# New TensorE piece lengths in an attention planner, and expert 0's block 10 finished in the next stage's order

## The chip, the cores and the metric

The kernel runs on one core of one Trainium2 chip. The metric is device time in microseconds (us) from one launch, the median of several runs. The core's engines each follow their own list of instructions in order: TensorE (PE in the profile, with its weight loads as PEld), VectorE (DVE), ScalarE (ACT), GpSimd (POOL) and SyncE (SP), which here only issues DMA transfers.

## The reference, cut to what matters

Three layers follow each other. Inputs are q, k, v and f_logit of shape (4, 8, 768, 48); all is fp32.

```python
f = 1.0 / (1.0 + np.exp(-f_logit))
for t in range(S):
    state = f[:, :, t, :, None] * state + np.einsum('bhd,bhe->bhde', k[:, :, t], v[:, :, t])
    y[:, :, t] = np.einsum('bhd,bhde->bhe', q[:, :, t], state)
# x = y as (3072, 384)
logits = x @ w_gate
P = np.exp(logits - logits.max())
for _ in range(8):
    P /= P.sum(1, keepdims=True) + 1e-09
    P /= P.sum(0, keepdims=True) + 1e-09
    P *= N / E
for e in range(E):                      # 8 experts, F = 1024
    out += P[:, e:e + 1] * (np.maximum(x @ w1[e], 0.0) @ w2[e])
# second layer: (x @ w_a) * (x @ w_b) @ w_out, inner width 1536
```

The normalisation of P runs over all 3072 tokens, so no expert's result can be weighted before the last token's gate logits are known.

## The kernel before, in words

**Two stages.** The attention stage works through 24 steps of 128 tokens (function `attention`, `NSTEP = 24`). The main stage then does the experts (`front`, `back`), and after them the second layer, over three groups of 1024 tokens. Products are fp32 precision made of fp32r pieces: each operand is split into a high part and a low part, and a product takes three matmuls.

**A step of attention.** TensorE's part is a row of short pieces: three transposes of f, q and k (`tr`, L463), the score products `m0`, `m8`, `m16`, `m32` (L506, L518, L557, L570) over blocks of growing width, a transpose of k (`kt`, L582), two state updates (`kv`, L607) and the output (`ym`, L641). Between them VectorE scales q and k for the next level (L529, L531, L577), copies the finished scores under a mask (L550 after `m0`, L543 after the others), and keeps the state (L632, L634). The order of adding makes the first of the copies at L543 wait for `m16`, which writes the same bank as `m8`. ScalarE does the exponentials of f (L468 to L473), copies k (L588), copies the state into place (L622) and moves `ym`'s result out (L650). SyncE rearranges that result into x (L657, six small transfers), and ScalarE and VectorE split x into its high and low part (L670, L671). Two sets of buffers let one step overlap the next.

**Filling work.** While attention waits, TensorE runs expert 0 on blocks of 256 tokens as soon as their two steps are done (function `expert0`): first seven products x times w1 of nine matmuls of 256 columns each (L326), then two products h times w2 of 21 matmuls of 384 columns each (L338), whose results ScalarE moves out (L721) and stores (L723). Below the nine-matmul groups are called F and the 384-column matmuls G. There are twelve blocks. Blocks 0 to 10 are planned into the attention stage as filling work, block 11 into the main stage, since its x comes last. The gates (`logits`, six small matmuls at L681 and a reduction at L686) follow each step's x; the last step's gates are planned into the main stage, where the normalisation of P (`sinkhorn`, L752 to L776) waits for them.

**What sets the order.** A class `Plan` takes every operation with a priority, an engine, a cost, and the keys that it reads and writes. `order` then lists the operations by a time that it keeps for each engine: an operation becomes ready when those that it depends on have ended, plus a gap, and each engine takes the ready one of best priority. In the attention stage TensorE alternates between attention's pieces and filling work: each attention piece of cost c adds `SHARE * c` to an account and each filling piece takes its cost from it; a switch to filling work costs `TURN` more. The order of every engine's list in each stage comes from this one pass; each stage has its own `Plan` and starts its times at zero.

```python
plan.add(prio, PE, .75, [f"x{s % 4}", "wgs"], [kl], lambda: lg(psl))
...
op(PE, .53 * n, hk + wk, [km, "E0o"], partial(
    gemm_t, psm[:, :DM], hs[fs], ws[fs], tt * 128, part == 0, part == 3), 0.0, fill)
...
if i % 2 == 1 and i + 1 < NSTEP:
    expert0(plan, i // 2, 1000 * (i + 1), "M", p_M, True)
...
logits(plan, NSTEP - 1, -4000, "R", p_R[:2])
expert0(plan, NSTEP // 2 - 1, E0_AT, "R", p_R[:2], False)
```

The last two lines are the head of the main stage's list. `x_take` there loads further sums of x (`z<-xf0d` on SyncE), splits them on ScalarE (`xsh`) and on VectorE or GpSimd (`xsl`).

Of the kernel before, what the change touches and what calls it, by code (L numbers as in the profile page):

```python
# [84 lines left out]
class Plan:  # L85
# [6 lines left out]
    GAP = 0.2  # L92
    MOST, DEBT = 2.0, 0.9
    SAME = 0.13
    TURN = 0.19
    COLD = 10.0

    def __init__(self, gap=GAP, hold=GAP, same=SAME, over=0.0):
# [25 lines left out]
    def order(self, share):  # L124
# [56 lines left out]
def kernel(  # L181
# [249 lines left out]
    def attention(s):  # L431
# [34 lines left out]
        op(PE, .44, [f"natf{z}"], [kf], lambda: tr("f", psf))  # L466
# [8 lines left out]
        op(PE, .44, [f"natq{z}"], [kq], lambda: tr("q", psq))  # L475
        kk_, psk = take("T", p_T)
        op(PE, .44, [f"natk{z}"], [kk_], lambda: tr("k", psk))
# [30 lines left out]
        op(PE, 1.1, [bqk, bkk], [a0k], m0)  # L508
# [13 lines left out]
        op(PE, .95, [f"q3{z}", f"k3{z}"], [a1k], m8)  # L522
# [38 lines left out]
        op(PE, .85, [f"q3{z}", f"k3{z}"], [a1k], m16)  # L561
# [11 lines left out]
        op(PE, .73, [f"q3{z}", f"k3{z}"], [a1k], m32)  # L573
# [11 lines left out]
        op(PE, .46, [f"k3{z}"], [ko], lambda: kt(pso))  # L585
# [28 lines left out]
        for c in range(2):  # L614
            kc, psc = take("O", p_O)
            op(PE, .55, [knk, f"vn{z}"], [kc], lambda c=c, psc=psc: kv(c, psc))
# [31 lines left out]
        op(PE, 1.2, [f"Xq{z}", f"Xa{z}", f"Yv{z}", f"Ys{z}"], [ky], lambda: ym(psy))  # L648
# [25 lines left out]
    def logits(plan, s, prio, nm, bufs):  # L674
# [10 lines left out]
        plan.add(prio, PE, .75, [f"x{s % 4}", "wgs"], [kl], lambda: lg(psl))  # L685
# [3 lines left out]
    def expert0(plan, b, prio, nm, bufs, fill):  # L689
# [7 lines left out]
        for ft in range(NF0):  # L697
# [13 lines left out]
        for tt in range(EB // 128):  # L711
            km, psm = take(nm, bufs)
            for part in range(4):
                n = min(2, NF0 - 2 * part)
                hk = [f"h{x}{ft}" for ft in range(part * 2, part * 2 + n) for x in "hl"]
                fs = slice(part * 2, part * 2 + n)
                wk = [f"e0o{part // 2}{x}" for x in range(e0_f[part // 2])]
                op(PE, .53 * n, hk + wk, [km, "E0o"], partial(
                    gemm_t, psm[:, :DM], hs[fs], ws[fs], tt * 128, part == 0, part == 3), 0.0, fill)
# [59 lines left out]
    for i in range(NSTEP):  # L779
# [3 lines left out]
        if i % 2 == 1 and i + 1 < NSTEP:  # L783
            expert0(plan, i // 2, 1000 * (i + 1), "M", p_M, True)
# [328 lines left out]
    w2d = {}  # L1113
    logits(plan, NSTEP - 1, -4000, "R", p_R[:2])
# [100 lines left out]
```

## Time and profile before

| what | value |
|---|---|
| median of 3 runs | 2245.74 us (2245.48 to 2248.01) |
| the profiled execution, its own time | 2248.24 us |
| its span, first to last instruction | 2246.5 us |
| PE, PEld, DVE, ACT, POOL busy | 97%, 88%, 74%, 44%, 43% of the span |
| TensorE's granted clock, mean | 0.987 |
| chain that ended last | PE 82%, DVE 9%, DMA 4%, ACT 2% |

The profile counts an engine as busy while an instruction of its own runs; a granted clock of 1.00 is the higher of TensorE's two levels (2.4 GHz), 0.50 the lower (1.2 GHz). The shares are means over two stages with different limits, so the sections below read each stage by itself.

### The profile page before, as it was taken

The page shows a single profiled execution, that of the slowest core. Times are in us where ns is not written, and L with a number is a line of the kernel's source. Part 1 is how long each engine was busy: PE and PEld are TensorE (multiplying, and loading weights), DVE is VectorE, ACT ScalarE, POOL GpSimd, SP SyncE. Part 2 cuts the span into 40 slices and gives each one's busy share as a digit, 9 for nine tenths or more (in the row PEclk, how much of TensorE's full clock was granted, in tenths as well). Part 3 has the DMA queues.
Part 4 walks back from the last instruction along what each step waited for, and adds up shares of the span by engine and source line. Part 5 has one row for each costly group of instructions (what it writes and reads, how often), then busy time and mean ns, then how long its engine had stood idle before and what let it go on. Part 6 is the DMA issues. An engine that isn't in the chain of part 4 may idle for free.

```text
span 2246.5 us, 41073 instructions
## 1 busy us (share of the span) xinstructions
PE 2188.3 (97%) x15333; PEld 1969.1 (88%) x15333; DVE 1666.5 (74%) x2948; ACT 990.3 (44%) x1921; POOL 964.3 (43%) x982
## 2 busy tenths in 40 slices
PE   8998999989999999999999999999999999999999
PEld 8897888877899999879999999899999998888888
DVE  6888888868778777767677777777767767766655
ACT  4554555554444444443333344443433445433432
POOL 2214344249776665333322234443222487444512
PEclk9999999999999999999999999999999999999999
DMA  7455644256665556874544457676444456687742
GB/s 135 88 104 151 159 90 97 60 202 235 234 238 176 198 189 233 300 253 167 189 164 168 146 183 252 238 237 222 157 168 150 162 176 225 239 281 232 249 139 75
DMA packets 325353, 413.39 MB, mean 184 GB/s; under 512 B 146976, under 2 KB 217248, under 8 KB 321696
## 3 DMA queue, kind: packets, MB, share of 16 engines
q1 hardware_dynamic: 321216, 405.84, 56.5%
q10 hardware_dynamic: 3936, 4.92, 0.6%
q8 instruction: 121, 1.98, 0.4%
q14 instruction: 80, 0.66, 0.1%
HBM read 279.33 MB, written 126.62 MB: 181 GB/s over the span
## 4 chain that ended last, share of the span: by engine, by line
PE 82%; DVE 9%; DMA 4%; ACT 2%; issue 1%; SPq 1%; POOL 1%; DVEq 0%; ACTq 0%; POOLq 0%
PE pR L338 37%; PE pG L981 25%; PE pF L981 9%; PE pM L338 2%; PE pM L326 2%; DVE fi L486 1%; PE pA L506 1%; DVE X L543 1%; DMA wd<-z 1%; PE pA L518 1%; PE pT L463 1%; DVE z L1174 1%; PE pO L641 1%; DMA w<-wfmoe 1%; PE pA L557 1%
## 5 line engine op out<-in xcount | busy, mean ns | idle before, releaser
L338 PE MATMUL pR<-er 128*128 128x384 f32 x5010 | 1012.8, 337 | 3.5 <-DVE acc L1174 1.5
L338 PEld LDWEIGHTS pR<-er 128*128 128x128 f32 x5010 | 897.7, 188 | 77.6 <-DVE acc L1174 2.9
L1174 POOL TENSOR_TENSOR er<-z,er 128x512 fp32r<-128x512 f32 x221 | 295.4, 1349 | 625.4 <-ACT er L1174 389.4
L1174 ACT ACTIVATE z<-pG 128x512 f32<-128x512 f32 x474 | 282.9, 598 | 556.1 <-PE pG L981 455.1
L981 PE MATMUL pG<-xsh,w 128*128 128x512 f32 x1134 | 442.7, 397 | 10.8 <-ACT z L1174 10.5
L1174 DVE SCALAR_TENSOR_TENSOR acc<-pR,prob,acc 128x384 f32<-128x384 f32 x528 | 319.2, 612 | 120.9 <-PE pR L338 118.7
L1174 ACT ACTIVATE er<-z 128x512 fp32r<-128x512 f32 x420 | 250.7, 626 | 220.6 <-PE pR L338 192.1
L1174 DVE TENSOR_TENSOR z<-pF,z 128x512 f32<-128x512 f32 x324 | 221.6, 687 | 113.3 <-PE pF L981 82.1
L981 PE MATMUL pG<-er,w 128*128 128x512 f32 x972 | 277.9, 395 | 2.1 <-DVE z L1174 2.0
L981 PEld LDWEIGHTS pG<-xsh,w 128*128 128x128 f32 x1134 | 213.4, 188 | 49.2 <-ACT z L1174 16.8
L1174 DVE TENSOR_TENSOR z<-z,pG 128x512 f32<-128x512 f32 x243 | 166.6, 686 | 118.4 <-PE pG L981 114.7
L981 PE MATMUL pG<-xsl,w 128*128 128x512 f32 x567 | 224.7, 396 | 0.0
L981 PEld LDWEIGHTS pG<-er,w 128*128 128x128 f32 x972 | 178.9, 188 | 27.2 <-DVE z L1174 5.4
L1174 DVE TENSOR_TENSOR z<-pG,z 128x512 f32<-128x512 f32 x174 | 119.7, 688 | 85.7 <-PE pG L981 82.5
L707 POOL TENSOR_TENSOR er<-l,er 128x256 fp32r<-128x256 f32 x84 | 72.4, 864 | 234.3 <-ACT l L705 208.2
L1174 DVE SCALAR_TENSOR_TENSOR er<-z,er 128x512 fp32r<-128x512 f32 x171 | 165.4, 975 | 6.9 <-ACT er L1174 4.9
L1174 POOL TENSOR_TENSOR stage<-stage 128x128 f32<-128x128 f32 x325 | 160.2, 525 | 17.3 <-DMA stage<-wd 7.9
L1174 POOL TENSOR_TENSOR w<-stage,w 128x768 fp32r<-128x768 f32 (+2 forms) x75 | 122.5, 1644 | 81.8 <-ACT w L1174 74.9
L981 PE MATMUL pF<-er,w 128*128 128x512 f32 x486 | 139.4, 395 | 1.2 <-DVE z L1174 0.8
L296 POOL TENSOR_TENSOR er<-raw,er 128x384 fp32r<-128x384 f32 (+1 forms) x82 | 91.9, 1126 | 84.9 <-ACT er L294 77.2
L981 PE MATMUL pF<-xsh,w 128*128 128x512 f32 x324 | 127.4, 396 | 0.5 <-DMA w<-wfmoe 0.4
L1174 POOL TENSOR_TENSOR l<-l,l 128x512 f32<-128x512 f32 x60 | 83.5, 1398 | 91.6 <-DMA l<-x2d 48.5
(167 smaller groups left out, 2738.4 us busy)
## 6 DMA issues: line engine op xcount, KB each, us to landing
er<-w2d SPq DMA_DIRECT2D x138, 384.0 KB, 5.4
wfmoe<-w SPq DMA_DIRECT2D x19, 1920.0 KB, 8.0
w<-wfmoe SPq DMA_DIRECT2D x38, 768.0 KB, 6.1
w2d<-er SPq DMA_DIRECT2D x69, 384.0 KB, 4.9
w<-wfmoe SPq DMA_DIRECT2D x38, 640.0 KB, 4.5
w<-wfmoe SPq DMA_DIRECT2D x38, 512.0 KB, 4.1
wfout<-w SPq DMA_DIRECT2D x8, 1920.0 KB, 7.3
raw<-in_moe_w_dram SPq DMA_DIRECT2D x64, 192.0 KB, 2.8
```

The costliest lines, as they stand in the source:

```text
L296: plan.add(prio + 1, "POOL", .1 + m * .0026, [gk, key], [key], lambda: nc.gpsimd.tensor_tensor(out=lj, in0=got, in1=f32(hj), op=ALU.subtract))
L326: nc.tensor.matmul(out=ps, lhsT=a[:, kk, fs], rhs=b[:, kk, :], start=(i == 0), stop=(i == 3 * KD - 1),)
L338: nc.tensor.matmul(out=ps, lhsT=a[:, off:off + 128], rhs=b, start=(start and i == 0), stop=(stop and i == n - 1))
L463: nc.tensor.transpose(ps[0:R, p * 128:p * 128 + 128], src[:, p * 128:p * 128 + R], ident)
L486: op(DVE, .71, [], [f"fi0{z}", f"fi1{z}"], lambda a=a, c=c: nc.vector.tensor_tensor(out=fi[:, :, :, a], in0=fi[:, :, :, a], in1=fi[:, :, : ...
L506: nc.tensor.matmul(out=A0[o:o + 64, g, :], lhsT=pct(bk)[r:r + D, g, :], rhs=pct(bq)[r:r + D, g, :])
L518: nc.tensor.matmul(out=A1[o:o + 56, 0, g, :].rearrange("j (b e) -> j b e", e=8), lhsT=pct(k3)[r:r + D, g, 0:56], rhs=qv[r:r + D, g, :, 1, :])
L543: nc.vector.copy_predicated(X[r, hd].rearrange("j g (b two e) -> j g b two e", two=2, e=n)[:, :, :, 1, :], mbc(r, o, nb, n), A1[r, lv].rea ...
L557: nc.tensor.matmul(out=A1[o:o + 48, 1, g, :].rearrange("j (b e) -> j b e", e=16), lhsT=pct(k3)[r:r + D, g, 0:48], rhs=qv[r:r + D, g, :, 1, :])
L707: op(POOL, .76, [f"hh{ft}", kf], [f"hl{ft}"], lambda hh=hh, hl=hl, hf=hf: nc.gpsimd.tensor_tensor(out=hl, in0=hf, in1=f32(hh), op=ALU.subt ...
L981: nc.tensor.matmul(out=ps, lhsT=a[:, slot], rhs=b, start=(new and i == 0), stop=(i == 2), skip_group_check=not new)
L1174: fn()
```

## The change

Three things are changed. The cost that the planner gives to each of TensorE's pieces in attention is replaced by another number, lower in all cases, and `TURN` goes from 0.19 to 0.17. The second half of expert 0's block 10 (its 42 G) leaves the attention stage's list and is added at the head of the main stage's list. There an operation of no instruction on an engine of its own, named "clock", tells the planner that the last step's x is ready 8.0 after the stage's start. A way to rank operations (`ranked`) is added to the class and not used. The body of `expert0` takes a parameter `part` that picks its first half (0), its second (1) or both.

```diff
-    TURN = 0.19
+    TURN = 0.17
...
-        op(PE, .44, [f"natf{z}"], [kf], lambda: tr("f", psf))
+        op(PE, .41, [f"natf{z}"], [kf], lambda: tr("f", psf))
...
-        op(PE, 1.1, [bqk, bkk], [a0k], m0)
+        op(PE, 1.0, [bqk, bkk], [a0k], m0)
...
-        op(PE, .95, [f"q3{z}", f"k3{z}"], [a1k], m8)
+        op(PE, .91, [f"q3{z}", f"k3{z}"], [a1k], m8)
...
-        op(PE, .85, [f"q3{z}", f"k3{z}"], [a1k], m16)
+        op(PE, .84, [f"q3{z}", f"k3{z}"], [a1k], m16)
...
-        op(PE, .73, [f"q3{z}", f"k3{z}"], [a1k], m32)
+        op(PE, .63, [f"q3{z}", f"k3{z}"], [a1k], m32)
...
-        op(PE, .46, [f"k3{z}"], [ko], lambda: kt(pso))
+        op(PE, .32, [f"k3{z}"], [ko], lambda: kt(pso))
...
-            op(PE, .55, [knk, f"vn{z}"], [kc], lambda c=c, psc=psc: kv(c, psc))
+            op(PE, .44, [knk, f"vn{z}"], [kc], lambda c=c, psc=psc: kv(c, psc))
...
-        op(PE, 1.2, [f"Xq{z}", f"Xa{z}", f"Yv{z}", f"Ys{z}"], [ky], lambda: ym(psy))
+        op(PE, 1.05, [f"Xq{z}", f"Xa{z}", f"Yv{z}", f"Ys{z}"], [ky], lambda: ym(psy))
...
-        plan.add(prio, PE, .75, [f"x{s % 4}", "wgs"], [kl], lambda: lg(psl))
+        plan.add(prio, PE, .69, [f"x{s % 4}", "wgs"], [kl], lambda: lg(psl))
...
-        for ft in range(NF0):
+        for ft in range(NF0) if part != 1 else ():
...
-        for tt in range(EB // 128):
+        for tt in range(EB // 128) if part != 0 else ():
...
-            expert0(plan, i // 2, 1000 * (i + 1), "M", p_M, True)
+            expert0(plan, i // 2, 1000 * (i + 1), "M", p_M, True, 0 if i + 3 > NSTEP - 1 else None)
...
+    plan.add(-9000, "clock", 8.0, [], [f"x{(NSTEP - 1) % 4}"], lambda: None)
+    expert0(plan, NSTEP // 2 - 2, -8000, "R", p_R[:2], False, 1)
     logits(plan, NSTEP - 1, -4000, "R", p_R[:2])
```

Code of the change stands eight to ten lines further down than before (L338 is L346, L681 is L689, L1174 is L1184).

**TensorE at the end of attention, before.** `pM` and `pO` are PSUM banks of the attention stage, `pR` and `pG` of the main stage; the rows run from the last gates in attention to the first work of the main stage.

```order
L338 MATMUL pM_159<-er 128x384 x6
L641 MATMUL pO_156<-X_126,Y_124 48x64 x16
L338 MATMUL pM_159<-er 128x384 x9
L681 MATMUL pR_6465<-wgs,er 128x16
...
L981 MATMUL pG_6460<-xsh_73,w_83 128x512
L981 MATMUL pG_6460<-xsl_74,w_83 128x512
L981 MATMUL pG_6460<-xsh_73,w_83 128x512
L326 MATMUL pR_6466<-er 128x256 x9
L754 MATMUL pR_6467<-ident,sk_m_68 1x128
```

**The same place now.**

```order
L649 MATMUL pO_156<-X_126,Y_124 48x64 x16
L346 MATMUL pR_6420<-er 128x384 x21
L346 MATMUL pR_6421<-er 128x384 x21
L989 MATMUL pG_6415<-xsh_73,w_83 128x512
...
L989 MATMUL pF_6417<-xsh_79,w_83 128x512
...
L689 MATMUL pR_6420<-wgs,er 128x16
...
L334 MATMUL pR_6421<-er 128x256 x9
L334 MATMUL pR_6420<-er 128x256 x9
L762 MATMUL pR_6422<-ident,sk_m_68 1x128
```

The G stand behind the last `ym` (L649) in two banks, six matmuls of the main stage follow, and then the last gates. After the gates two F of block 11 use the two banks again, ahead of the first matmul of the normalisation.

**VectorE at the last gates, before.**

```order
L671 TENSOR_TENSOR er<-xf_138,er 128x3x128
L686 TENSOR_REDUCE logit<-pR_6465 128x8
L752 TENSOR_REDUCE sk_m_68<-logit 128x1
L755 TENSOR_REDUCE sk_m_69<-pR_6467 1x1
...
L769 RECIPROCAL sk_r<-sk_r 128x24
L1174 TENSOR_TENSOR xsl_6488<-z_6473,xsh_6487 128x512
```

**VectorE and, behind it, ScalarE at the same place now.**

```order
L679 TENSOR_TENSOR er<-xf_138,er 128x3x128
L1184 TENSOR_TENSOR xsl_6443<-z_6428,xsh_6442 128x512
L1184 TENSOR_TENSOR xsl_6447<-z_6430,xsh_6446 128x512
L1184 TENSOR_TENSOR xsl_6449<-z_6431,xsh_6448 128x512
L694 TENSOR_REDUCE logit<-pR_6420 128x8
L760 TENSOR_REDUCE sk_m_68<-logit 128x1
```

```order
L678 ACTIVATE er<-xf_138 128x3x128
L1184 ACTIVATE xsh_6442<-z_6428 128x512
L1184 ACTIVATE xsh_6444<-z_6429 128x512
L1184 ACTIVATE xsh_6446<-z_6430 128x512
L1184 ACTIVATE xsh_6448<-z_6431 128x512
L729 ACTIVATE l_90<-pR_6421 128x384
```

Three subtractions for the loaded sums moved ahead of the gates' reduction on VectorE, and four casts ahead of the move of bank `pR_6421` on ScalarE.

**VectorE in a step of attention, before (step 13).** The rows run from the scaled k, on which `m16` waits, to the copy that waits for `m16`.

```order
L550 COPY_PREDICATED X_126<-mask,pA_157 64x512 x2
L529 TENSOR_TENSOR q_133<-q_133,g_143 112x32x8
L531 TENSOR_TENSOR k_135<-k_135,g_143 112x32x8
L543 COPY_PREDICATED X_126<-mask,pA_158 56x32x8
L529 TENSOR_TENSOR q_133<-q_133,g_145 112x16x16
```

**The same step now.**

```order
L558 COPY_PREDICATED X_126<-mask,pA_157 64x512
L537 TENSOR_TENSOR q_133<-q_133,g_143 112x32x8
L539 TENSOR_TENSOR k_135<-k_135,g_143 112x32x8
L558 COPY_PREDICATED X_126<-mask,pA_157 64x512
L486 TENSOR_TENSOR fi_127<-e_129,fi_127 112x512
L488 SCALAR_TENSOR_TENSOR fi_127<-fi_127,e_129 112x512
L551 COPY_PREDICATED X_126<-mask,pA_158 56x32x8
```

One of the two copies of `m0`'s scores and two operations of the next step (`fi_127`) now stand between the scaled k and the waiting copy (L551, formerly L543).

## Rows read from the trace of the kernel before

**Rows 1.** Stretches: length, busy PE, PEld, DVE, ACT, POOL, then clock, DMA, GB/s.
```profile
15.00:457.00 442.00, 415.66 (x6443) 375.17 (x6443) 375.75 (x821) 235.13 (x589) 137.03 (x146) 0.96 0.50 108
457.00:475.00 18.00, 12.76 (x74) 10.74 (x68) 4.55 (x11) 7.23 (x15) 2.03 (x2) 0.81 0.71 226
475.00:535.00 60.00, 54.70 (x254) 43.53 (x255) 55.44 (x110) 33.06 (x68) 52.87 (x66) 0.99 0.72 255
700.00:2246.00 1546.00, 1529.96 (x7677) 1378.67 (x7675) 1103.16 (x1814) 637.62 (x1116) 642.09 (x602) 1.00 0.59 200
```
**Rows 2.** VectorE's waits from 15 to 457 us: total, times, longest.
```profile
DVE X L543 <- PE pA L557: 25.5, 22, 2.7
```
**Rows 3.** VectorE's timeline in one step: start, us, what, idle before.
```profile
145.60 0.44 DVE L543 COPY_PREDICATED X<-mask,pA 56x256 f32<-56x256 int32 x1 [1.20 <-PE pA L557]
```
**Rows 4.** TensorE's timeline at the end of attention.
```profile
443.00 1.31 PE L326 MATMUL pM<-er 128*128 128x256 f32 x9
...
447.33 2.35 PE L338 MATMUL pM<-er 128*128 128x384 f32 x12
449.62 0.70 PE L570 MATMUL pA<-q,k 48*32 48x32 f32 x32
...
451.40 0.55 PE L582 MATMUL pO<-ident,k 112*128 112x112 f32 x4
...
453.48 0.94 PE L607 MATMUL pO<-vn,kn 64*64 64x48 f32 x32
...
456.27 1.10 PE L641 MATMUL pO<-X,Y 128*48 128x64 f32 x32
...
463.78 0.38 PE L681 MATMUL pR<-wgs,er 128*128 128x16 f32 x1 [4.65 <-ACT er L670]
```
**Rows 5.** VectorE's timeline, then ScalarE's, in the last step of attention.
```profile
448.72 0.40 DVE L531 TENSOR_TENSOR k<-k,g 112x256 f32<-112x256 f32 x1
...
450.36 0.44 DVE L543 COPY_PREDICATED X<-mask,pA 48x256 f32<-48x256 int32 x1 [0.46 <-PE pA L570]
450.83 0.42 DVE L577 TENSOR_TENSOR k<-k,g 112x256 f32<-112x256 f32 x1
...
451.62 0.54 DVE L671 TENSOR_TENSOR er<-xf,er 128x384 fp32r<-128x384 f32 x1
454.20 0.35 DVE L634 TENSOR_TENSOR S<-S,pO 112x192 f32<-112x192 f32 x1 [2.03 <-PE pO L607]
...
452.21 0.55 ACT L588 ACTIVATE kn<-pO 128x448 f32<-128x448 f32 x1
...
454.58 0.75 ACT L622 ACTIVATE Y<-S 64x192 f32<-64x192 f32 x2 [1.21 <-DVE S L634]
```
**Rows 6.** SyncE's issues around x, then one transfer's median to landing (455 to 480 us).
```profile
463.20 0.37 SPq L666 DMA_DIRECT2D x1d<-xf  x1
463.62 1.92 SPq L1174 DMA_DIRECT2D z<-xf0d  x4
...
z<-xf0d SPq DMA_DIRECT2D x8, 256.0 KB, 4.4
```
**Rows 7.** VectorE's timeline, then ScalarE's, after the last gates.
```profile
465.64 0.17 DVE L686 TENSOR_REDUCE logit<-pR 128x8 f32<-128x16 f32 x1 [1.32 <-PE pR L681]
...
471.86 0.35 DVE L766 TENSOR_REDUCE sk_r<-prob 128x24 f32<-128x192 f32 x1 [0.43 <-ACT prob L762]
...
473.12 0.69 DVE L1174 TENSOR_TENSOR xsl<-z,xsh 128x512 fp32r<-128x512 f32 x1 [0.36 <-ACT xsh L1174]
...
475.12 2.38 DVE L1174 TENSOR_TENSOR xsl<-z,xsh 128x512 fp32r<-128x512 f32 x2
...
472.47 2.18 ACT L1174 ACTIVATE xsh<-z 128x512 fp32r<-128x512 f32 x4
```
**Rows 8.** Busy time by stretch, as in rows 1, where the granted clock fell.
```profile
68.00:77.00 9.00, 9.00 (x119) 8.29 (x120) 7.23 (x18) 4.57 (x15) 3.07 (x4) 0.62 0.12 24
463.70:469.00 5.30, 5.01 (x20) 4.53 (x20) 1.09 (x3) 0.63 (x2) 0.00 (x0) 0.50 0.94 289
```

More of the change, by code (lines that the diff above doesn't have):

```diff
@@ L94, with __init__ @@
     SAME = 0.13
-    TURN = 0.19
+    TURN = 0.17
     COLD = 10.0
-    def __init__(self, gap=GAP, hold=GAP, same=SAME, over=0.0):
+    def __init__(self, gap=GAP, hold=GAP, same=SAME, over=0.0, ranked=False):
+        self.ranked = ranked
         self.gap, self.hold, self.same, self.over = gap, hold, same, over
@@ L137, in order @@
                 todo.setdefault(o[1], []).append(n)
+        if self.ranked:
+            rank = [0.0] * len(self.ops)
+            for n in range(len(self.ops) - 1, -1, -1):
+                o = self.ops[n]
+                far = o[5] + max((rank[u] + (self.gap if self.ops[u][1] != o[1] else 0.0) for u in users[n]), default=0.0)
+                rank[n] = o[2] + far
+            self.ops = [(o[0] if o[0] == 10 ** 9 else -r, *o[1:]) for o, r in zip(self.ops, rank)]
         free, made = {}, []
@@ L684, in logits, with expert0 @@
         kl, psl = take(nm, bufs)
-        plan.add(prio, PE, .75, [f"x{s % 4}", "wgs"], [kl], lambda: lg(psl))
+        plan.add(prio, PE, .69, [f"x{s % 4}", "wgs"], [kl], lambda: lg(psl))
         plan.add(prio, DVE, .16, [kl], [f"lg{s}"], lambda: nc.vector.tensor_reduce(
             out=logit[:, s, :], in_=psl[:, :2 * E].rearrange("p (two e) -> p e two", two=2), axis=AX.X, op=ALU.add))
-    def expert0(plan, b, prio, nm, bufs, fill):
+    def expert0(plan, b, prio, nm, bufs, fill, part=None):
         def op(*a):
@@ L710, in expert0 @@
         ws = ftiles(w_e0[0][1]) + ftiles(w_e0[1][1])
-        for tt in range(EB // 128):
+        for tt in range(EB // 128) if part != 0 else ():
             km, psm = take(nm, bufs)
[L713 to L717, printed above, removed]
+            for n0 in range(4):
+                n = min(2, NF0 - 2 * n0)
+                hk = [f"h{x}{ft}" for ft in range(n0 * 2, n0 * 2 + n) for x in "hl"]
+                fs = slice(n0 * 2, n0 * 2 + n)
+                wk = [f"e0o{n0 // 2}{x}" for x in range(e0_f[n0 // 2])]
                 op(PE, .53 * n, hk + wk, [km, "E0o"], partial(
-                    gemm_t, psm[:, :DM], hs[fs], ws[fs], tt * 128, part == 0, part == 3), 0.0, fill)
+                    gemm_t, psm[:, :DM], hs[fs], ws[fs], tt * 128, n0 == 0, n0 == 3), 0.0, fill)
             ys, ky = b_ys[tt % 2], f"l{1 + tt % 2}"
```

4 lines of the change are left out of this document (2 added, 2 removed).

## The prediction

> **What bounds the kernel now.** I read the busy time by stretch first [rows 1]. From 700 us on TensorE is busy for 1529.96 of 1546 us at full clock: that part can only be moved as a whole. By the order of the program it also holds the same work in the same sequence after the change. From VectorE's 1113th of 2950 instructions on, near 670 us, and TensorE's 5213th of 13022, the lists agree except for PSUM bank numbers. So whatever is won or lost before arrives undiminished at the end.
>
> From 15 to 457 us, attention, no engine is full: TensorE 415.66 and VectorE 375.75 of 442 us, which is 17.3 and 15.7 us a step over 24 steps, in steps of about 18. The two pass work to and fro, and what costs time is each one's waiting for the other. VectorE's largest wait is the masked copy L543 that waits for `m16`, 25.5 us in 22 cases, 1.16 each [rows 2]; [rows 3] is one such case. From 457 to 475 us TensorE sits idle, 4.65 us of it in one piece: the last gates wait for x, which SyncE rearranges [rows 4]. The clock is at 0.50, its lower level, for the 5.3 us behind that hole [rows 8]. From 475 to 535 us VectorE (55.44 of 60 us) and GpSimd (52.87) set the pace, not TensorE [rows 1].
>
> **Part 1, attention's new order.** No instruction is added except one dummy matmul at the start. What counts is which work stands in the waits. In the list before, VectorE has nothing between the scaled k and the copy that waits for `m16` in 13 of 24 steps, one short operation in 8 or 9, and enough to cover the wait in two. In the new list, 12 steps have enough there (step 13 is shown above), ten have one short operation and one has nothing. So ten more steps cover a wait of 1.16 us [rows 2]: **-11.6 us** at most. The other bound is zero, if VectorE then waits elsewhere: the operations now in the gap came from places where they covered something else.
>
> Against this, filling work is spread less evenly. Step 7 now gets 54 F matmuls and 18 G, step 6 only 9 and 21; before it was 45 and 12, and 18 and 24. A matmul of F takes 0.14 us (1.25 us to the next piece for 9) and one of G 0.19 (2.29 for 12) [rows 4]. All filling in attention is then 693 x 0.14 + 462 x 0.19 = 185 us. Of the 415.66 us some 15 are dummies at the start, so attention's own pieces take about 9 us a step. The four lightest steps of the new list (4, 6, 12 and 18) then need 14.5, 14.2, 15.5 and 15.5 us of TensorE, less than VectorE's 15.7: TensorE idles there for 3.1 us that it must make up in heavy steps. Before, from step 3 on, the lightest steps need 16.1, and idle none by this sum. **+3.1 us**, with bounds zero and twice that.
>
> Light steps also leave `kt` and `kv` without filling work between them in steps 6, 12, 18 and 23, where formerly there always was some. Holes can cost clock: from 68 to 77 us the granted clock was 0.62 after TensorE had waited [rows 8], a loss of 0.38 x 9 = 3.4 us. There are six such stretches in attention after the start. I take half a stretch more, **+1.7 us**, between three fewer (-10) and three more (+10).
>
> **Part 2, the tail of attention.** Before, 33 of block 10's 42 G stand between `m16` and the last `ym`, and nine behind it [rows 4]. Without them TensorE waits for VectorE and ScalarE instead. `m32` follows one F where 12 G took 2.29 us; its last operand, k, was scaled by 449.12 [rows 5], so it can start 0.5 us before 449.62. From `m32`'s start to `ym`'s start it was 6.65 us. The new chain is: `m32` 0.70; on VectorE a copy 0.44, the low part of x 0.54, a copy 0.44, k 0.42; `kt` 0.55, its copy 0.55, half of `kv` 0.47, state 0.35, its copies 0.75. That is 5.21, and ten hand-overs of 0.05 (from 450.80 to 450.83 and the like) make 5.7 [rows 4, 5]. So `ym` ends 0.5 + 1.0 = **1.5 us earlier**, and x with it.
>
> **Part 3, the transition.** Call the end of the last `ym` zero; before it is 457.37. x lands and SyncE goes on at 463.20, that is at 5.8 [rows 6]. TensorE now has 42 G (8.0 at 0.19) and six main-stage matmuls (1.4) in that time, reaching the gates at 9.4 and finishing them near 10.2, where it finished them at 8.2 before. The hole of 4.65 us is filled.
>
> But a new wait is put behind it. VectorE has three subtractions ahead of the gates' reduction, and ScalarE four casts ahead of the move that frees bank `pR_6421`; both need sums that SyncE only issues after x. The planner starts all engines of this stage at zero; its "clock" delays x but not these loads. The fourth load is issued 1.44 us after 463.62 and takes 4.4 to land [rows 6]: 469.5, or 12.1 from `ym`. A cast (0.55) and a subtraction (0.69) later [rows 7] VectorE reaches the reduction at about 13.4, which before ran at 8.3 [rows 7]. TensorE stops too: its F behind the gates needs `pR_6421`, free near 13.2, so some 3 us idle replace the 4.65, and the clock can fall again.
>
> The normalisation so begins 5.1 us later after `ym`, 3.6 later in all, since `ym` is 1.5 sooner. In return the three subtractions (0.69 + 2.38 us [rows 7]) are already done; before they stood inside the normalisation, in a stretch where VectorE is full. Two F stand ahead of the normalisation's first matmul; with half of them at the lower clock they take 1.25 us longer, of which I take half, 0.6. Sum: 3.6 - 3.1 + 0.6 = **+1.1 us**. Bounds: below, the new wait costs nothing, and both the 1.5 and half of the 5.3 us at the lower clock are won, -4.2; above, the subtractions would have been hidden anyway, +4.2.
>
> VectorE's list is in order: that is why it sat 1.20 us before the masked copy with other work behind it [rows 3]. The Trainium skill (page "TensorE: Matmul & The Clock Gate", section "Architectural detail: the array is 16× 32×32, not 1× 128×128") says that ScalarE and VectorE take their queues strictly first in, first out, and only TensorE's weight loads are pulled ahead. By it the reduction cannot pass the subtractions, and Part 3 stands at +1.1; if it could, Part 3 would be -4.2. The trace agrees where it shows the case.
>
> **Sum.** -11.6 + 3.1 + 1.7 + 1.1 = -5.7 us. The profiled execution took 2248.24, so its like would take 2242.5. It lies 2.5 us above the median of the runs shown, 2245.74; for the median I forecast 2245.7 - 5.7 = **2240 us**. A measurement of this kernel can tell about 0.2%, 4.5 us, from no change: faster is below 2241.2, slower above 2250.2.
>
> **Rivals.** *The hole is simply paid back.* TensorE's 9.4 us of work covers x's 5.8, the loads land sooner than 4.4, and the clock stays up. Part 3 is then -4.2, the sum -11.0, 2234.7 us. For it: the hole and its slow 5.3 us are plain in [rows 4, 8]. Against it: the loads' landing time. The Trainium skill's same page, section "HAM oscillation — how this bites in real kernels", holds that bursts of matmuls parted by waits run at the lower clock again and again, and advises an order that keeps TensorE at work through the wait; the trace agrees on the clock behind this hole. Chance 0.18.
>
> *Another wait takes the place of the covered one.* Only a third of the 11.6 us is kept: -3.9 + 3.1 + 1.7 + 1.1 = +2.0, 2247.7 us. For it: TensorE is as near to full in attention as VectorE, so a covered VectorE wait need not move TensorE. Against it: 25.5 us is the largest wait of the stage. Chance 0.24.
>
> *The bare pieces cost clock; slower.* The place is `kt` and `kv` of steps 6, 12, 18 and 23. If two more stretches like the one at 68 us follow, they cost 6.8; with half of the cover, -5.8 + 3.1 + 6.8 + 1.1 = +5.2, 2250.9 us. It decides from the second extra stretch on. For it: the stage's mean clock is already 0.96 [rows 1]. Against it: the holes before falls were in heavy steps too, and the new order may cover some. Chance 0.15.
>
> **How the numbers follow.** My forecast has 0.43; its own range is 2235 to 2244. Of it 0.30 lies in faster, 0.12 in no change, 0.01 in slower. The paid hole gives 0.17 faster and 0.01 no change; the moved wait 0.03, 0.18 and 0.03; the lost clock 0.03 no change and 0.12 slower. Together faster 0.50, same 0.34, slower 0.16. Full cover with the paid hole and none of the charges would be -15.8, 2230; the range goes from there to the slower rival, 2251, and leaves out more than one extra slow stretch beyond it.
>
> **What would show it.** Attention: the last `ym` starts near 448 instead of 456.27, and the wait of L543 (now L551) for `m16` falls from 25.5 us towards 14. Transition: no idle of TensorE before the gates, but some 3 us behind them at the next F, released by ScalarE's move of the bank; the gates' reduction on VectorE 13 us after `ym`'s end. If that reduction comes at 10, Part 3 is wrong and the first rival right. If the wait for `m16` falls and the last `ym` does not come earlier, the second is. If the mean clock from 15 to 457 us is below 0.95, the third is. From 700 us to the end nothing should change but the start.

## The result and the profile after

The changed kernel took 2272.06 us (median of 4 runs, 2259.75 to 2278.12), the kernel before in the same session 2245.61. The ratio is 1.0117, interval 1.0089 to 1.0144: 26 us slower (1.2%), outside the forecast range. The profiled execution took 2272.82 us, with a span of 2271.0 and a mean granted clock of 0.983 (before 0.987).

Busy time by stretch, after: length, busy PE, PEld, DVE, ACT, POOL, then clock, DMA, GB/s. These answer to [rows 1].

```profile
15.00:469.00 454.00, 413.36 (x6396) 372.49 (x6397) 379.09 (x821) 238.20 (x588) 139.13 (x146) 0.94 0.48 105
470.40:491.40 21.00, 18.34 (x92) 17.28 (x93) 4.22 (x10) 8.84 (x19) 4.00 (x4) 0.80 0.68 229
491.40:557.80 66.40, 56.47 (x262) 43.97 (x260) 57.21 (x111) 31.95 (x62) 53.16 (x66) 1.00 0.65 234
728.00:2271.00 1543.00, 1525.38 (x7644) 1375.41 (x7643) 1095.67 (x1808) 635.49 (x1113) 636.83 (x600) 1.00 0.58 199
```

Attention has 42 G fewer and yet lasts longer, at a clock of 0.94 instead of 0.96. The rounds of the normalisation (third row) leave VectorE idle for 9 of 66 us. The last row is as before. The loss lies ahead of it, and in three pieces:

| from, to | before, us | after, us |
|---|---|---|
| start to the end of the last `ym` | 457.4 | 470.4 |
| from there to the first row sum (L766, now L774) | 14.5 | 21.0 |
| from there to the first accumulation of an expert's result | 59.6 | 66.4 |

These are two single executions, and attention's time varies by itself: in eleven profiles of kernels whose lists agree up to the last step, the last `ym` but one ends between 434.3 and 444.4 us (442.4 in the kernel before). In the change and three relatives with the same order up to there it ends between 452.4 and 457.9 us, so the loss is real, but its 13 us are known only to within several us.

VectorE's waits from 15 to 469 us, after; the first row answers to [rows 2].

```profile
DVE X L551 <- PE pA L565: 10.5, 12, 1.8
DVE X L558 <- PE pA L514: 9.2, 10, 2.0
DVE logit L694 <- PE pO L689: 8.0, 8, 1.9
DVE q L537 <- PE pA L526: 7.7, 9, 1.7
DVE fi L486 <- ACT e L481: 6.4, 4, 1.9
```

The wait for `m16` fell from 25.5 to 10.5 us, more than forecast. But the four others shown grew, by 18 us in all: for `m0` from 6.1, for the gates from 1.7, for `m8` from 5.3, and the fifth wasn't there. VectorE's busy time hardly changed; it waits elsewhere, and idles for 75 us of this stretch where it idled for 66 [rows 1]. On TensorE, after and then before:

```profile
PE pO L590 <- DVE k L585: 10.8, 11, 2.5
PE pO L615 <- ACT kn L596: 7.8, 8, 2.3
PE pT L471 <- ACT bq L504: 5.4, 2, 3.1
PE pA L578 <- DVE k L539: 4.4, 5, 2.5
```
```profile
PE pO L582 <- DVE k L577: 6.2, 9, 1.3
PE pO L607 <- ACT kn L588: 2.9, 3, 2.3
PE pT L463 <- ACT e L468: 0.7, 1, 0.7
PE pA L570 <- DVE k L531: 0.8, 2, 0.5
```

The same four pieces (`kt`, `kv`, a transpose, `m32`) wait for 28 us in place of 11: the new list often has no filling work ahead of them. Behind three of these holes the clock falls (timeline, then stretches):

```profile
98.49 0.69 PE L578 MATMUL pA<-q,k 48*32 48x32 f32 x32 [2.46 <-DVE k L539]
443.56 0.60 PE L590 MATMUL pO<-ident,k 112*128 112x112 f32 x4 [1.84 <-DVE k L585]
464.34 0.60 PE L590 MATMUL pO<-ident,k 112*128 112x112 f32 x4 [2.46 <-DVE k L585]
```
```profile
98.50:107.50 9.00, 8.08 (x100) 7.35 (x102) 7.36 (x17) 3.92 (x12) 1.46 (x2) 0.62 0.29 57
444.00:452.00 8.00, 8.00 (x85) 7.46 (x85) 5.75 (x14) 4.53 (x14) 1.46 (x2) 0.57 0.02 4
464.00:473.00 9.00, 8.03 (x85) 7.57 (x86) 0.81 (x3) 3.20 (x7) 0.00 (x0) 0.62 0.03 6
```

The transition, TensorE and then VectorE, answering to [rows 4, 7]:

```profile
468.43 1.95 PE L649 MATMUL pO<-X,Y 128*48 128x64 f32 x32
470.31 8.28 PE L346 MATMUL pR<-er 128*128 128x384 f32 x42
...
479.82 0.73 PE L689 MATMUL pR<-wgs,er 128*128 128x16 f32 x6
483.21 4.21 PE L334 MATMUL pR<-er 128*128 128x256 f32 x18 [2.66 <-ACT l L729]
```
```profile
480.36 0.69 DVE L1184 TENSOR_TENSOR xsl<-z,xsh 128x512 fp32r<-128x512 f32 x1 [2.92 <-ACT xsh L1184]
482.12 1.74 DVE L1184 TENSOR_TENSOR xsl<-z,xsh 128x512 fp32r<-128x512 f32 x2 [1.07 <-ACT xsh L1184]
483.78 0.16 DVE L694 TENSOR_REDUCE logit<-pR 128x8 f32<-128x16 f32 x1
```

The hole of 4.65 us is filled and one of 2.66 us stands behind the gates; the reduction comes 13.4 us after `ym`'s end (470.38). Both are as forecast. `ym` itself takes 1.95 us instead of 1.10; it stands in the last stretch above, with a clock of 0.62.

### The profile page after: what moved, and what is told of

Its sections match the earlier page's. It is cut to its first block, busy times and chain, and to the rows that moved or that the text cites. A ratio compares the mean times of both kernels' runs of the same rounds, so it can differ in the third digit from the quotient of the medians.

```text
span 2271.0 us, 41053 instructions
## 1 busy us (share of the span) xinstructions
PE 2194.4 (97%) x15334; PEld 1974.8 (87%) x15334; DVE 1669.9 (74%) x2948; ACT 995.5 (44%) x1921; POOL 962.8 (42%) x982
## 4 chain that ended last, share of the span: by engine, by line
PE 81%; DVE 11%; DMA 3%; ACT 2%; issue 1%; SPq 1%; POOL 0%; DVEq 0%; ACTq 0%; POOLq 0%
PE pR L346 37%; PE pG L989 26%; PE pF L989 9%; PE pM L346 2%; DVE fi L494 1%; PE pM L334 1%; DVE X L551 1%; PE pO L649 1%; PE pM L736 1%; PE pT L471 1%; PE pA L514 1%; DVE z L1184 1%; DMA wd<-z 1%; DVE er L1184 1%; PE pO L615 1%
## 5 line engine op out<-in xcount | busy, mean ns | idle before, releaser
L346 PE MATMUL pR<-er 128*128 128x384 f32 x5052 | 1021.7, 338 | 4.9 <-DVE acc L1184 2.9
L346 PEld LDWEIGHTS pR<-er 128*128 128x128 f32 x5052 | 906.2, 189 | 79.3 <-DVE acc L1184 4.7
L1184 POOL TENSOR_TENSOR er<-z,er 128x512 fp32r<-128x512 f32 x221 | 293.2, 1339 | 630.3 <-ACT er L1184 393.8
L1184 ACT ACTIVATE z<-pG 128x512 f32<-128x512 f32 x474 | 283.1, 598 | 556.3 <-PE pG L989 445.1
L989 PE MATMUL pG<-xsh,w 128*128 128x512 f32 x1134 | 441.1, 396 | 13.7 <-ACT z L1184 13.5
L1184 DVE SCALAR_TENSOR_TENSOR acc<-pR,prob,acc 128x384 f32<-128x384 f32 x528 | 318.7, 611 | 119.5 <-PE pR L346 114.6
L1184 ACT ACTIVATE er<-z 128x512 fp32r<-128x512 f32 x420 | 250.7, 626 | 219.3 <-PE pR L346 189.7
L1184 DVE TENSOR_TENSOR z<-pF,z 128x512 f32<-128x512 f32 x324 | 221.6, 687 | 118.7 <-PE pF L989 85.3
L1184 DVE TENSOR_TENSOR z<-z,pG 128x512 f32<-128x512 f32 x243 | 166.6, 686 | 120.5 <-PE pG L989 116.7
L1184 DVE TENSOR_TENSOR z<-pG,z 128x512 f32<-128x512 f32 x174 | 119.8, 689 | 87.8 <-PE pG L989 84.6
L1184 POOL TENSOR_TENSOR stage<-stage 128x128 f32<-128x128 f32 x325 | 159.6, 522 | 22.9 <-DMA stage<-in_moe_w_dram 12.9
L1184 DVE SCALAR_TENSOR_TENSOR er<-z,er 128x512 fp32r<-128x512 f32 x171 | 165.1, 974 | 4.5 <-ACT er L1184 2.2
L1184 POOL TENSOR_TENSOR w<-stage,w 128x768 fp32r<-128x768 f32 (+2 forms) x75 | 124.3, 1668 | 75.6 <-ACT w L1184 72.3
L1184 POOL TENSOR_TENSOR l<-l,l 128x512 f32<-128x512 f32 x60 | 81.3, 1362 | 89.8 <-DMA l<-x2d 51.9
```

Of the source, the lines that this page charges most:

```text
L346: nc.tensor.matmul(out=ps, lhsT=a[:, off:off + 128], rhs=b, start=(start and i == 0), stop=(stop and i == n - 1))
L989: nc.tensor.matmul(out=ps, lhsT=a[:, slot], rhs=b, start=(new and i == 0), stop=(i == 2), skip_group_check=not new)
L1184: fn()
```

## Experiments

All were timed beside the kernel before (medians of 2243.6 to 2244.9 us in the several sessions). "Clock loss" is (1 - mean granted clock) x span, averaged over a kernel's runs; "rest" is the span without it. Across the first 16 runs of the kernel before the time rises by 0.91 us per us of clock loss (0.72 to 0.95 in the later sessions), so the two columns part a slowdown, roughly, into clock and everything else. A kernel's mean clock loss is known to about 1 or 2 us; smaller differences in that column say nothing.

| run | us | ratio (interval) | clock loss | rest |
|---|---|---|---|---|
| before | 2244 | 1 | 24 to 26 | 2217 to 2218 |
| the change | 2272.1 | 1.0117 (1.0089, 1.0144) | 37 | 2231 |
| e1 lengths alone | 2263.5 | 1.0087 (1.0067, 1.0107) | 36 | 2225 |
| e2 move alone | 2254.8 | 1.0053 (1.0035, 1.0072) | 33 | 2221 |
| e3 move, loads told late | 2256.5 | 1.0056 (1.0034, 1.0078) | 32 | 2223 |
| e4 change, loads told late | 2270.7 | 1.0122 (1.0100, 1.0144) | 38 | 2231 |
| e5 move without "clock" | 2254.5 | 1.0038 (1.0021, 1.0055) | 29 | 2222 |
| e6 move, SyncE told busy | 2253.0 | 1.0033 (1.0016, 1.0050) | 30 | 2220 |
| e8 lengths and dummies | 2264.0 | 1.0091 (1.0069, 1.0114) | 27 | 2235 |
| e9 e5 and dummies | 2253.0 | 1.0042 (1.0025, 1.0060) | 24 | 2227 |
| f2 TURN .17 alone | 2252.6 | 1.0034 (1.0015, 1.0053) | 30 | 2221 |
| f4 lengths, TURN .21 | 2243.4 | 0.9995 (0.9979, 1.0011) | 24 | 2218 |
| f5 lengths, TURN .28, SHARE .68 | 2246.1 | 1.0006 (0.9987, 1.0024) | 22 | 2223 |
| f7 change, TURN .21 | 2250.3 | 1.0032 (1.0013, 1.0051) | 25 | 2224 |
| e10 one product moved | 2251.6 | 1.0022 (1.0000, 1.0044) | 24 | 2224 |
| e11 e10, lists kept | 2241.8 | 0.9990 (0.9970, 1.0011) | 23 | 2217 |
| f6 f4 and e11 | 2242.2 | 1.0002 (0.9984, 1.0020) | 22 | 2219 |
| e13 both moved, lists kept | 2249.0 | 1.0019 (1.0004, 1.0034) | 31 | 2217 |
| e14 "clock" alone | 2247.7 | 1.0013 (0.9997, 1.0029) | 24 | 2224 |

### Which part of the change costs

e1 has the new lengths and TURN, e2 the old ones with the move and "clock". e3 and e4 are e2 and the whole change with one edit, meant to bring the gates' reduction ahead of the subtractions:

```diff
+    plan.add(-9000, "clock2", 6.0, [], [...], lambda: None)   # read by the z loads
```

> Only the new piece lengths and TURN; block 10's G back in attention, no clock operation. Theory A (two causes of like size: attention's new order, and the transition): the last ym starts 11 to 13 us later than before, the transition is as before, time 12 us above before (about 2257). Theory B (attention's order is all of it, the transition only follows): 22 us or more above before. Theory C (the moved half block is all of it): within 4 us of before.

> Only the move of block 10's G behind the last ym with the clock operation; old piece lengths and TURN. Theory A: attention as before up to the last step, then 10 to 13 us lost between the last ym and the end of the normalisation, time about 2257. Theory B: within 4 us of before. Theory C: 20 us or more above before.

> As the move alone, and the planner is told that SyncE's first loads of the main stage start 6.0 late (they wait for x): the gates' reduction stands ahead of the three subtractions on VectorE, the move of the second bank ahead of the casts on ScalarE. Theory A1 (the loss of the transition comes from the reduction waiting for the loads): the hole of TensorE behind the gates goes, the reduction comes near 10 us after ym's end instead of 13.4, and 6 us or more of the move's loss is won back (about 2250). Theory A2 (it comes from the bare last step, its fall of the clock, and the later start of everything): within 3 us of the move alone.

> The whole change with the loads told as in the run before. Theory A1: 6 us or more below the change (about 2265). Theory A2: within 3 us of the change (2272).

Each part alone is slower with an interval clear of 1, by 19.5 and 11.9 us; the sum of the two, 31 us, lies within what the interval of the whole change allows (20 to 32). So there are two causes, as theory A has it, but not of like size: it gave the lengths 12 us, and their 19.5 are nearer to theory B. Of the 19.5 us, 10.8 are clock loss and 8.7 rest; of the 11.9, 7.4 and 4.6. By the time alone A2 holds for e3 and e4, but they are no test of the reduction: the planner put eight loads of `acc` and six of weights ahead of the loads on SyncE, so the reduction came earlier (10.2 us after `ym`'s end), but in e3 ScalarE then waited 9.24 us for the loads and TensorE 8.00. A wait was moved.

### The lengths, or the order that came out of them

By TensorE's list, the pieces and filling of a step add up to a time (durations from the trace). I summed what steps 3 to 23 lack to 15.5 us: 7.6 before, 15.7 with the new lengths and TURN .17, 4.5 with TURN .21, 23.9 with TURN .17 and the old lengths. These sums hang on the durations put in: with 8.3 us of attention's own work a step and the prediction's prices of F and G, the same lists give 0.4, 5.3, 1.4 and 11.1. Only the ranking of the two worst is firm.

```diff
-    TURN = 0.17
+    TURN = 0.21        # f4; f5: TURN .28 and SHARE .68; f2: TURN .17, old lengths
```

> Before with TURN .17 alone; all lengths old, nothing moved. By the order, TensorE's work in the lightest steps of attention (from the fourth on) then falls short of 15.5 us a step by 23.9 us in all; it is 7.6 in the kernel before and 15.7 with the new lengths and TURN .17. Theory 'uneven filling': the time follows that sum, so this kernel is slower than with the new lengths, 2260 to 2272, although no length is changed. Theory 'wrong lengths': without the new lengths the time stays near before, 2242 to 2250.

> All new lengths, but TURN .21 instead of .17; nothing moved. The order that comes out fills the steps evenly: the lightest fall short of 15.5 us by 4.5 us in all. Theory 'uneven filling': the loss of 19.5 us goes; the time is 2238 to 2248. Theory 'wrong lengths': the new lengths themselves put the filling at the wrong pieces, and at least half of the loss stays, 2254 or more.

> All new lengths, TURN .28 and SHARE .68; nothing moved. Lightest steps fall short by 3.7 us in all, but 12 m32 and 16 m16 of 21 follow another piece of attention directly, without filling (before: 8 and 11). Theory 'uneven filling': 2237 to 2248. Rival 'bare pieces': the number of pieces without filling ahead of them counts, not the evenness of the steps; then slower than before by 5 us or more.

f4 has every new length in place and differs from e1 in TURN alone, and the loss of 19.5 us is gone. So the lengths by themselves do no harm; what costs is the order that the planner makes of these lengths and TURN .17 together. (The new lengths with the old TURN, .19, were not run.) Attention in f4 (stretch, VectorE's wait for `m16`, then TensorE's waits):

```profile
15.00:450.00 435.00, 406.00 (x6425) 370.21 (x6426) 375.11 (x821) 233.75 (x589) 133.15 (x146) 0.97 0.50 110
```
```profile
DVE X L551 <- PE pA L565: 13.1, 14, 2.9
```
```profile
PE pA L565 <- DVE k L539: 7.7, 6, 4.1
PE pO L590 <- DVE k L585: 7.6, 7, 2.0
PE pA L578 <- DVE k L539: 3.4, 6, 1.0
...
PE pO L615 <- ACT kn L596: 2.7, 4, 1.4
```

The same waits in e1:

```profile
PE pO L590 <- DVE k L585: 8.0, 10, 1.8
PE pO L615 <- ACT kn L596: 6.0, 7, 1.6
PE pT L471 <- ACT bq L504: 5.4, 2, 3.1
PE pA L578 <- DVE k L539: 4.9, 4, 2.5
```

From e1 to f4 `kv`'s wait falls from 6.0 to 2.7 us and the transposes' goes; `kt`'s hardly changes, and `m16`'s grows from 1.6 to 7.7. The clock stands at 0.97. Against e1 (420.25 us busy and 34.75 idle from 15 to 470 us) the same work is 14 us shorter in busy time and 6 in idle: most of the loss was the lower clock. f4 also tells what the cover was worth: VectorE's wait for `m16` is 13.1 us there, nearly as short as in the change, and yet the time is that of the kernel before.

f5 has 12 `m32` and 16 `m16` without filling ahead of them and is not slower by more than the noise, so their number isn't the cause; its rest is 5 us higher than before, and its clock loss 3 lower. f2 missed: 23.9 us by my sum, but 8 us slower, not 16 or more. The trace shows why the sum misleads there: f2's list leaves two F and all 42 G of block 10 behind the last `ym` by itself.

```profile
462.44 2.42 PE L326 MATMUL pM<-er 128*128 128x256 f32 x18
...
465.29 7.53 PE L338 MATMUL pM<-er 128*128 128x384 f32 x42
```

Its last `ym` ends at 462.5 us although 33 G and 18 matmuls of F fewer than before stand ahead of it, and from there to the first accumulation it takes 75.2 us, no longer than before. So uneven filling is the reading that fits f4 and e1, but my sum doesn't give the size of the loss, and it isn't shown that unevenness, rather than particular bare pieces, is what costs.

### Can the clock be bought back with dummies?

```diff
+            warm("kt")     # 20 dummy matmuls of 128 columns, in chosen steps
```

> New lengths alone (as in the run of the lengths alone, 2263.5), with 20 dummy matmuls of 128 columns put ahead of six pieces that the new order left bare of filling: m32 of step 4, kv of 6, 12 and 18, kt of 14 and 22. Theory 'clock': the falls of the granted clock at 100, 140, 290 and 444 us go, 4 to 10 us come back (2254 to 2260), and the deficit of clock falls from 36 to about 27 us. Theory 'waits': the dummies fill idle time only; the time stays within 3 us of 2263.5 or grows by up to 7, which is their own length (120 of 0.06 us).

> As the move without 'clock', with 50 dummy matmuls in the last step ahead of m32, kt, kv and ym. Theory 'bare tail': the fall of the clock at the end of attention goes, ym is 1.1 us long again, and 3 to 6 us come back against the move without 'clock'. Theory 'order made by clock': no difference over 2 us from the move without 'clock'.

In e8 the clock loss fell by 9 us, as the theory of the clock had it, and in its profile the falls near 100, 140, 290 and 444 us are gone; so the holes ahead of these six pieces did cost clock. But the rest grew by 10. Twenty dummies took 2.4 us, not 1.2, or 14.6 us for all, and their own length ate what they gave. e9's time is that of e5 within the noise, as the second theory has it, and `ym` still takes 1.95 us. In its profile the dummies did not hold the clock: it fell at 447.0 us and stayed at the lower level up to 464, though TensorE was busy nearly all the time.

```profile
444.90:460.40 15.50, 14.98 (x152) 14.33 (x150) 3.93 (x11) 3.25 (x8) 0.00 (x0) 0.57 0.05 14
```

This profile has the lowest clock of e9's seven runs, and over them the mean clock loss is 24 us, 4 less than in e5, with 4 us more of rest. So here too the dummies cost as much as they gave. Shorter rows of dummies were not run.

### Why the move costs

> Old piece lengths; block 10's 42 G behind the last ym as in the change, but without the operation 'clock', so the planner thinks x is there at once: the gates stand directly behind the 42 G, two subtractions (not three) ahead of the reduction. Theory 'order made by clock': what cost 11 us in the move alone is the order that 'clock' 8.0 makes (subtractions ahead of the reduction, front work between the rounds), so this kernel is within 4 us of before, reduction at most 9.5 us after ym's end, first row sum to first acc about 60 us as before. Theory 'bare tail': what costs is that the last step's short pieces run without the G between them at the lower clock; then ym is still 1.95 us long and the kernel 6 to 11 us slower than before.

> Old piece lengths, the move with 'clock', and SyncE told that it is busy for the first 6.0, so the loads' sums are planned late: reduction ahead of the three subtractions on VectorE, move of the second bank ahead of the casts on ScalarE, SyncE's order kept. Theory 'late reduction': reduction about 10.5 us after ym's end instead of 13.4, no hole behind the gates, and 4 to 8 us of the move's 11 come back (2247 to 2251 where before is 2244). Theory 'bare tail or front work between the rounds': the reduction comes early but the time stays within 3 us of the move alone (2252 to 2257).

By the times the second theory, the bare tail, holds in both. In e6 the reduction comes 10.2 us after `ym`'s end and no hole stands behind the gates, as meant; still it is 7 us slower than before. In e5 the reduction is late again (12.9). But the loss isn't where that theory has it: the last step is about as long as before (14.8 to 15.2 us against 15.0), while the time from `ym`'s end to the first accumulation is 84.9 us in e2, 85.7 in e5, 82.4 in e6, whatever is done to the reduction, against 74.1 before. Next I moved only the second product, its 21 G; e11 is e10 with the cost of the moved work hidden from the planner, so that the lists of VectorE and ScalarE behind `ym` stay as before; e13 moves both products in that way, and e14 moves nothing and adds only "clock".

```diff
-        for tt in range(EB // 128) if part != 0 else ():
+        for tt in range(EB // 128) if part is None else (part,):          # e10, e11
...
-            plan.add(prio, *a)
+            plan.add(prio, a[0], 0.0 if part == 1 else a[1], *a[2:])       # e11, e13
...
-            km, psm = take(nm, bufs)
+            km, psm = take(nm, bufs) if part is None else (f"pR{2 - tt}", bufs[2 - tt])   # e13
```

> Old lengths; of block 10's two products h times w2 only the second (21 G, 4.0 us) goes behind the last ym, without 'clock'. Theory 'work taken from a free place' (TensorE idles in attention anyway, so 42 G leaving it shorten it by 1 to 2 us only, while behind ym they cost their whole 8 us less the 4.9 us of idle): 24 G then fit into the 5.8 us in which x travels, the reduction stays 8.3 to 9 us after ym's end, and the time is 2241 to 2247, within 0.2% of before. Theory 'any move costs' (the last step's pieces are left bare, the banks or the order behind them decide): 4 to 10 us slower than before.

> As the move of one product (21 G behind the last ym), but the planner is told that these 21 G and their moving out cost nothing, so VectorE's and ScalarE's lists behind ym stay as in the kernel before (no subtraction ahead of the first row sum). Theory 'order after the move': first row sum 14 to 15 us after ym's end (17.5 in the run with cost told), first row sum to first acc about 64; time 2241 to 2246, within 0.2% of before. Rival 'G behind ym cost in themselves': again about 2250.

> Old lengths, all 42 G behind the last ym, planned at no cost and in two other banks, so the lists of VectorE and ScalarE behind ym stay as in the kernel before; the gates stand behind 42 G. Theory 'G beyond the hole are paid in full': the gates wait for 8 us of G instead of 5.8 us of x, so the reduction comes 10.5 to 11 us after ym's end, 2 to 3 us later than before; less 1 to 2 us by which attention ends sooner the time is 2242 to 2247, within 0.2% of before. Rival 'the 42 G in themselves cost the 10 us': 2250 to 2256.

> Old lengths, nothing moved, only the operation 'clock' 8.0 added: 27 matmuls of the main stage stand ahead of the gates, four VectorE operations ahead of their reduction. Theory 'the order that clock makes costs': the reduction again 13 us or more after ym's end, first acc 81 us or more after it (74 to 79 without 'clock'), time 2248 to 2256. Rival 'the moved G cost, clock is harmless': within 4 us of before, 2240 to 2248.

e10 was expected to cost nothing; its median is 8 us longer, by the ratio 5, with an interval that just reaches 1. Its profile is one of its two fastest runs (2242.5 us, attention ended at 447.6), but the loss shows in it all the same: 84.6 us from `ym`'s end to the first accumulation. Its reduction was on time (8.4 us after `ym`'s end), but the planner, told of 4 us more on TensorE, had put three subtractions into the chain ahead of the first row sum:

```profile
459.91 3.50 DVE L1183 TENSOR_TENSOR xsl<-z,xsh 128x512 fp32r<-128x512 f32 x3
463.33 0.14 DVE L767 COPY sk_mb<-pR 128x1 f32<-128x1 f32 x1
```

With the lists kept (e11), the same 21 G cost nothing, and the stretch takes 76.0 us; e10 and e11 differ in the lists alone, and in rest by 7 us. With all 42 (e13) it is 4 us, between what the two theories gave, and the two columns say of what kind: the rest is that of before, the clock loss 5 to 7 us more. Much of that clock is lost in attention's last step, here in the kernel before, e11, e13 and e2, between the ends of its last two `ym`:

```profile
442.38:457.37 14.99, 14.99 (x229) 13.62 (x228) 6.48 (x16) 6.18 (x16) 2.20 (x3) 1.00 0.16 42
```
```profile
436.28:449.58 13.30, 12.98 (x216) 11.77 (x216) 6.48 (x16) 6.17 (x16) 2.20 (x3) 1.00 0.18 47
```
```profile
436.95:452.32 15.37, 11.88 (x196) 10.73 (x195) 6.46 (x16) 5.78 (x15) 2.18 (x3) 0.72 0.12 28
```
```profile
441.52:456.31 14.79, 11.10 (x195) 10.11 (x195) 6.45 (x16) 5.78 (x15) 2.19 (x3) 0.82 0.13 29
```

With 21 G taken out the step is 1.7 us shorter, at full clock. With 42 out it is as long as with them: TensorE waits, the clock falls, and the pieces on the path run slower. This is no chance of one execution: `ym` takes 1.95 us in all nine profiles of kernels that have the 42 G moved, and 1.10 or 1.25 in the other eleven, f2 among them, where F stands between the last pieces. e13's profile shows its time behind `ym`, though: 80.4 us to the first accumulation.

e14 is the other half: clock loss as before, rest 6 us more, first accumulation 83.9 us after `ym`'s end. But its median, 3 us longer, lies where the rival had it, the interval takes in 1, and the profile is of its second slowest run. So by e14's time a cost of the order alone is not shown; the stretch behind `ym` and e10 against e11 speak for it.

### Do the two causes hang together, and does a mended version win?

> The whole change with TURN .21 in place of .17, nothing else. Theory 'two causes that add up' (uneven filling by TURN .17 with these lengths; 42 G and the order that 'clock' makes behind ym): only the move's cost is left, 2251 to 2258. Rival 'they need each other': near the whole change, over 2262.

> The new lengths with TURN .21 (2243.4 alone) and the 21 G behind ym at no told cost. If both parts are free of their cost and the hole of 4.65 us behind ym is used, 2237 to 2243; if the G behind ym cost in themselves, 2247 to 2252.

> The kernel before, unchanged, for a second profile: last ym's end to first acc was 74.1 us in the first profile, 77.4 to 78.7 in three kernels whose main stage has the same list. If 74.1 is chance, the second profile lies between 75 and 79; if the list is what makes it, at 73.5 to 75.

f7, the whole change but for TURN .21, keeps only the move's cost, 7 us, a little under what I expected; from `ym`'s end to the first accumulation it takes 87.7 us. f6 has the new lengths, TURN .21 and one product moved with the lists kept: it equals before. So both losses can be taken away, and no gain is left to measure: the 4.65 us of idle behind `ym`, filled to about half here (2.7 are left), bring less than the noise.

The second profile of before gave 75.7 us from `ym`'s end to the first accumulation, where the first gave 74.1. By the forecast that would be chance, but the forecast took two lists for one. The new cost of the gates also enters the main stage's plan, so with the new lengths VectorE's list differs from that of before from the third round on, even where nothing is moved. The twenty profiles fall into groups by that list:

| VectorE's list behind the last `ym` | profiles | `ym`'s end to first accumulation, us |
|---|---|---|
| as before | before (twice), e11, f2 | 74.1 to 76.0 |
| as before, 42 G moved | e13 | 80.4 |
| new lengths, move not told | e1, e8, f4, f5, f6 | 77.4 to 78.7 |
| move or "clock" told | the change, e2 to e6, e9, e10, e14, f7 | 82.4 to 93.3 |

Within a list the stretch varies by 1 to 2 us; between lists it moves by up to 19. e10 and e14 stand in the last row with 21 G moved and with none.

## Why the prediction was wrong

**Part 1** is the larger failure. The mechanism that it counted on took place, and to a larger extent: the wait for `m16` fell by 15 us, not 11.6. The step that failed is "-11.6 us at most": this was taken as the likely value, though TensorE was as near to full as VectorE; all of it came back as waits for `m0`, `m8`, the gates and the exponentials. f4 shows the same for an order without the other losses: its wait for `m16` is 12 us shorter than before, and it is no faster, with no more than 2 or 3 us given back behind `ym` (77.4 us against 74.1 to 76.0). And the charges were too small. For uneven filling I put +3.1; in e1 the rest grew by 8.7, a few us of it behind `ym`. (A reading was off here: the dummies from 15 to 457 us take 25 us, not 15, so attention's own pieces take some 8.3 us a step, not 9, and the term would have come out near +5.) For the clock I put +1.7, "half a stretch more", with a bound of +10; the clock loss grew by 10.8. The third rival had the mechanism and the places (`kt` and `kv` left bare), with 6.8 us for the clock. Its sign, a clock below 0.95 up to 457 us, is met or missed within the rounding: the profile shows 0.95 there, and 0.94 up to 469. The sign of the second rival came true as stated: the wait for `m16` fell, and the last `ym` came later.

**Part 2**, "1.5 us earlier", failed on the clock. In e2 `m32` starts 0.45 us earlier in the step, as forecast, and `ym` 1.05; but `ym` then takes 0.85 longer, and the step ends 0.2 us earlier in all. The chain of 5.7 us was built from pieces at full clock; without filling work the step's clock was 0.72 to 0.82. With half the G left in place 1.7 us were there (e11).

**Part 3** was right in what it could see: the reduction at 13.4 us after `ym`'s end, the hole of 4.65 us filled, the new one behind the gates 2.66 us where I said some 3. The VectorE queue went in order, as the Trainium skill says (page "TensorE: Matmul & The Clock Gate", section "Architectural detail: the array is 16× 32×32, not 1× 128×128"): the reduction passed none of the subtractions. The step that failed is "-3.1", the subtractions already done. It took VectorE for the engine that sets the pace in the rounds [rows 1]. In the change VectorE is busy for 57.2 us there, where it was 55.3 of 59.6, and idles for 9; in the first two rounds alone it waits 3.2 us for ScalarE (`z`), which it did not before. From the first row sum to the first accumulation it took 59.6 and 61.2 us in the two profiles before and 66.4 after: 6.8 longer, not 3.1 shorter. Why the told order is longer in these rounds is not taken apart further. Nor did the prediction price the 42 G themselves. That 8 us of G stand in 4.65 us of idle isn't what they cost: with VectorE's list kept, the first row sum comes 13.5 us after `ym`'s end in e13 and 15.5 in f2, against 14.5 before. They cost 4 us where taking them out leaves the last pieces bare (e13).

The first rival, the hole paid back, falls: the hole was filled in e6 without a new one behind the gates, and in part in e11 and f6, and it paid nothing measurable. The second, another wait in place of the covered one, had the mechanism, but let a third of the cover stay where none did. My forecast took each of these charges near its middle; they came together at their upper bounds or beyond.

What stays open: which of the uneven steps or bare pieces cost the 8.7 us that aren't clock; why TURN .17 with the old lengths costs only 8 us and with the new ones 19.5; and how the move's cost, 7 to 12 us in e2, e5, e6 and f7, splits between the G's effect (4, shown by e13) and the order that the planner makes when told (some 8 us behind `ym` in the traces of e10 and e14, but 3 in e14's time, not clear of noise).

## What to carry to other kernels

Filling work that stands in idle time is nearly free there: 42 G taken out of the last step shortened it by 0.2 us at most. Before moving such work into another hole, count what it covered where it was, by the pieces that will be left without it and by the clock that these then run at. A covered wait is worth something only if nothing else takes its place. A greedy planner's order can change from an early step to the end when one of its numbers changes by 0.02 (f2); judge the list that comes out (evenness of the steps, bare pieces, what stands ahead of the critical operation on each queue), not the truth of the numbers. When work is moved ahead of a planned stage, see whether the planner, told of it, reorders the engines that you did not mean to touch.

## What the runs showed of the hardware

VectorE's short operations can last as long as the GpSimd operation beside them (spans on GpSimd are rough in these profiles). In the rounds of e1 a scaling of 24 columns took 0.18 us while GpSimd idled and up to 1.50; the longest ended with GpSimd's (VectorE first, then GpSimd, which idled from 509.6 to 514.46):

```profile
508.29 1.29 DVE L775 TENSOR_SCALAR sk_r<-sk_r 128x24 f32<-128x24 f32 x1
513.53 0.18 DVE L775 TENSOR_SCALAR sk_r<-sk_r 128x24 f32<-128x24 f32 x1
...
538.11 1.50 DVE L775 TENSOR_SCALAR sk_r<-sk_r 128x24 f32<-128x24 f32 x1
```
```profile
508.26 1.29 POOL L1182 TENSOR_TENSOR w<-stage,w 128x512 fp32r<-128x512 f32 x1 [1.25 <-ACT w L1182]
514.46 1.02 POOL L304 TENSOR_TENSOR er<-raw,er 128x384 fp32r<-128x384 f32 x1 [4.91 <-ACT er L302]
...
538.04 1.54 POOL L1182 TENSOR_TENSOR w<-stage,w 128x640 fp32r<-128x640 f32 x1
```

The eight of them took 5.1 us in e1 and 2.4 before. Which of them meet a long GpSimd operation goes with the list: the last of the eight takes 1.50 or 1.51 us in all five profiles of the new lengths with the move not told, and 0.47 in the four with the list of before.

And of the clock: in e9's profile the dummies and short pieces kept TensorE busy for 14.98 of 15.50 us and the clock stood at 0.57; it rose at 464 us, within the 42 G that follow `ym`. In the kernel before, with G in place of the dummies, the last step ran at 1.00.
